# A fused attention and maxout FFN kernel: first loads through hardware queues with casts on chip, another pace for the FFN units, other PSUM banks

## The chip, the cores and the metric

The program runs on one core of one Trainium2 chip. The metric is the device time of one execution in microseconds (us), as a median of several runs. The "span" of a profiled run goes from its first to its last instruction; it is 1.7 us shorter than the time in the two profiled runs compared first, and 1.7 to 2.0 in the others.

Names: PE is the matrix engine (TensorE), DVE the vector engine, ACT the scalar engine (ScalarE), POOL is GpSimd, SP the sync engine. PE writes its sums into PSUM; the kernel's three PSUM pools below hold eight banks (3 + 2 + 3).

## The reference

```python
# q, k, v: 8 batches x 8 heads x 576 tokens x 64; beacon_k, beacon_v: 16 more keys per head
k_all = concat([beacon_k, k]); v_all = concat([beacon_v, v])        # 592 keys
scores = q @ k_all.T / 8, causal over the last 576 keys
a = exp(scores - max); a /= a.sum() + 1e-9
x = (a @ v_all), heads side by side                                  # 4608 tokens x 512
h = maximum(maximum(x @ w1, x @ w2), x @ w3)                         # 4608 x 768
out = h @ w_out                                                      # 4608 x 512, FP32
```

Inputs and output are FP32; the kernel computes in BF16 with FP32 sums.

## The kernel before

The program is a fixed order of instructions for each engine, written by one Python function. It works in these units:

- A *pair* is two heads of one batch: four pairs to a batch, 32 in all. Its scores are made in six *chunks* of key rows. In each chunk PE makes one score tile for each of the two heads, ACT takes the exponential, and DVE or POOL masks the diagonal.
- Before its first chunk, a pair's queries and keys are turned on PE (28 small transposes) and copied from PSUM by DVE into `qz` and `kT`.
- A *quad* is two pairs. Its *value passes* (six, in three steps) come in chunks 2 to 4 of the next quad's first pair.
- The FFN works on blocks of 512 tokens. A block has 22 *units*: 18 of the first layer (4 matmuls each) and 4 of the second (6 each). Units are laid between the chunks, so that PE has work while ACT makes exponentials. A block is ready only when the batch that it ends in has had its value passes.

The parts that matter here, with cuts marked:

```python
sc_psum  = ...tile_pool(name="sc_psum",  bufs=3, space=PSUM)   # scores and transposes
pv_psum  = ...tile_pool(name="pv_psum",  bufs=2, space=PSUM)
ffn_psum = ...tile_pool(name="ffn_psum", bufs=3, space=PSUM)
...
def load_qk(b, hs):                     # cast FP32 -> BF16 by the transfer, issued from GpSimd
    nc.gpsimd.dma_start(out=q_sb[:, hs, :], in_=q[b, hs]...)
    nc.gpsimd.dma_start(out=k_sb[BP:KP, hs, :], in_=k[b, hs]...)
    nc.gpsimd.dma_start(out=k_sb[0:BP, hs, :], in_=beacon_k[b, hs]...)
...
def emit_all():
    for pi in range(2): load_qk(0, ...pair pi...)
    for t in range(n_kt): load_v(0, t); build_mask(t)
    for pi in range(2, PPB): load_qk(0, ...)
    load_weights()                      # then batch 1: load_qk(1, all heads), load_v(1, t)
    ...
    emit_transposes(0)
    for p in range(NPAIR):
        b, pi = divmod(p, PPB)
        for c in range(6):
            emit_scores(p, c)
            if p >= 2 and p % 2 == 0 and 1 <= c <= 3:
                emit_pv(p // 2 - 1, c - 1)
            if c == 4 and pi == 0:
                ready = b - 1           # batch b - 1 is complete: its block may start
            if c == 4 and p + 1 < NPAIR:
                emit_transposes(p + 1)
            if b > 0:
                allowed += 0.95         # FFN units allowed so far
                while done[0] + 1 <= allowed and ... units[done[0]][0] <= ready:
                    emit_ffn(ready, allowed)
    # after the last pair: its quad's value passes, then all the units that are left
```

The softmax here doesn't subtract the row's maximum and nothing guards it: scores larger than these inputs give would overflow.

## Time and profile before

Time: 372.36 us (371.84 to 372.39), span 371.0 us. I cut the span at the first exponential of each batch, read in ACT's timeline:

| stretch | before, us |
|---|---|
| start to batch 0's first exponential | 8.8 |
| batch 0 | 36.0 |
| batch 1 | 37.6 |
| batches 2 to 7, mean of one | 39.7 |
| after the last exponential (44 units, last value passes, output) | 50.6 |

The page's second part of the kernel before has one digit for each fortieth of the span (9.3 us): the busy share of the engine in tenths (9 is 90% or more); for PEclk the clock that was granted to PE, in tenths of full speed; for DMA the mean share of the 16 transfer engines.

```profile
PE   2895499999999998989997999799998999899994
ACT  1754156645664666464746375555646365521110
PEclk9996599999999999989998999989998999999998
DMA  7999907761876168610953078703952001300404
```

PE is nearly always busy after 50 us, and the start is loaded with transfers. But a busy PE need not be a useful one. The chain of waits of the kernel before, in order of time (start, us, what), cut to where batches begin:

```profile
28.39 14.20 DMA k_sb<-in_beacon_k_dram
51.00 3.56 PE fps L300 x16
88.04 4.42 PE fps L300 x20
125.92 5.29 PE fps L300 x24
166.34 6.15 PE fps L300 x28
207.13 6.15 PE fps L300 x28
247.48 7.01 PE fps L300 x32
288.52 7.88 PE fps L300 x36
```

These are first-layer matmuls in one uninterrupted run: 4, 5, 6, 7, 7, 8 and 9 units. Each batch frees one block of 22 units, the pace is 24 chunks of 0.95, so 22.8. The units run out before a batch ends, 0.8 earlier each time, nothing is ready until the fifth chunk of the next batch, and then the allowance is caught up in one burst.

What PE does when units have run out is in the windows of the kernel before (stretch, its length, then busy time and number of instructions of PE, of PE's weight loads, of DVE, ACT and POOL, then the granted clock, where 1.00 is full, DMA share, GB/s). The first line is a stretch with units, for comparison:

```profile
188.00:190.00 2.00, 2.00 (x36) 1.24 (x35) 1.52 (x4) 0.58 (x2) 0.61 (x2) 1.00 0.00 0
198.00:200.00 2.00, 0.80 (x22) 0.46 (x15) 1.69 (x3) 0.50 (x3) 1.07 (x4) 1.00 0.71 227
200.00:202.00 2.00, 1.69 (x32) 1.06 (x34) 0.00 (x0) 1.38 (x5) 1.03 (x4) 0.74 0.00 0
202.00:204.00 2.00, 2.00 (x40) 0.97 (x36) 0.46 (x1) 1.72 (x4) 0.30 (x1) 0.50 0.00 0
```

PE idles 1.2 of 2 us, then its clock is halved, and in the last line it is "fully busy" at half the clock. The Trainium skill warns of this: "Perfetto Trace Analysis", in the note at its head, calls matmul busy time a bad metric for how close a kernel is to its limit.

Last, what PE waited for, from the waits of the kernel before (us in total, times, longest):

```profile
PE sc L176 <- DMA q_sb<-in_q_dram: 9.5, 2, 4.8
PE sc L215 <- DVE kT L193: 7.1, 9, 1.1
PE sc L215 <- ACT at_sb L223: 6.4, 20, 0.6
PE sc L184 <- DMA k_sb<-in_beacon_k_dram: 4.7, 2, 3.3
```

The first and last lines are the loads of batches 0 and 1. The third is a wait for a score bank that an exponential has still to empty.

### The profile page before, as it was taken

To read this page: it belongs to the slowest core of one execution; us is meant where nothing else is said; L and a number is where in the kernel's file an instruction comes from. 1 tells how busy PE (TensorE), PEld (TensorE's weight loads), DVE (VectorE), ACT (ScalarE), POOL (GpSimd) and SP (SyncE) were. 2 spreads that over 40 slices of the span, in tenths; PEclk is the share of its full clock that TensorE was granted. 3 is DMA by queue.
4 is the path that set the end of the run, shared out by engine and by line. 5 is a ranking of instruction groups with operands and counts; after the bars stand their busy time and mean duration, and the time that the engine had idled before them with its cause. 6 is when DMAs were issued, how large, how long until landed. Compare 5 with 4: busy or idle time off the path is not lost.

```text
span 371.0 us, 9819 instructions
## 1 busy us (share of the span) xinstructions
PE 333.5 (90%) x4064; PEld 178.9 (48%) x4064; DVE 185.9 (50%) x334; ACT 186.2 (50%) x503; POOL 163.9 (44%) x441
## 2 busy tenths in 40 slices
PE   2895499999999998989997999799998999899994
PEld 1452255545555555554554555354554555444441
DVE  3444156555646554545553656444563646245452
ACT  1754156645664666464746375555646365521110
POOL 8965127552765356533844165534654143300000
PEclk9996599999999999989998999989998999999998
DMA  7999907761876168610953078703952001300404
GB/s 78 128 186 204 137 4 116 59 104 35 122 52 110 30 98 79 96 44 7 155 48 104 2 110 67 137 2 43 133 81 59 0 2 31 87 2 0 113 2 113
DMA packets 60812, 27.64 MB, mean 75 GB/s; under 512 B 42976, under 2 KB 56160, under 8 KB 60768
## 3 DMA queue, kind: packets, MB, share of 16 engines
q0 software_dynamic: 55008, 17.58, 43.9%
q1 hardware_dynamic: 5760, 9.44, 9.1%
q8 instruction: 32, 0.52, 0.6%
q14 instruction: 12, 0.10, 0.1%
HBM read 35.13 MB, written 9.44 MB: 120 GB/s over the span
## 4 chain that ended last, share of the span: by engine, by line
PE 75%; ACT 7%; DMA 7%; POOL 6%; DVE 2%; issue 1%; POOLq 0%; ACTq 0%
PE fps L300 35%; PE fps L317 11%; PE sc L215 10%; PE pv L261 10%; PE sc L300 4%; ACT at_sb L223 4%; DMA k_sb<-in_beacon_k_dram 4%; PE sc L184 3%; PE sc L176 2%; DMA w_sb<-in_moe_w_dram 2%; PE sc L317 1%; POOL v_sb L137 1%; DVE kT L193 1%; ACT lnd L271 1%; DMA v_sb<-in_v_dram 1%
## 5 line engine op out<-in xcount | busy, mean ns | idle before, releaser
L223 ACT ACTIVATE at_sb<-sc 128x288 bf16<-128x288 f32 (+4 forms) x384 | 130.3, 404 | 91.4 <-PE sc L215 90.5
L239 POOL TENSOR_SCALAR_AFFINE_SELECT at_sb<-at_sb 128x57 bf16<-128x57 bf16 (+1 forms) x336 | 94.3, 300 | 145.2 <-ACT at_sb L223 139.7
L300 PE MATMUL fps<-xT,w_sb 128*128 128x512 bf16 x576 | 140.4, 380 | 0.0
L310 DVE TENSOR_TENSOR hT<-hT,fps 128x512 bf16<-128x512 bf16 x96 | 65.9, 686 | 56.9 <-PE fps L300 42.8
L300 PEld LDWEIGHTS <-w_sb 128*128 128x128 bf16 x648 | 59.5, 98 | 61.3 <-issue 0.8
L215 PEld LDWEIGHTS <-kT 128*128 128x128 bf16 (+1 forms) x384 | 36.6, 105 | 52.1 <-DVE kT L193 11.9
L308 ACT CAST hT<-fps 128x512 bf16<-128x512 f32 x48 | 28.1, 585 | 59.5 <-PE fps L300 49.5
L278 DVE TENSOR_TENSOR xT<-pv,recip 128x288 bf16<-128x288 f32 x64 | 27.5, 454 | 53.1 <-ACT recip L273 41.5
L317 PE MATMUL fps<-w_out_sb,hT 128*128 128x512 bf16 x192 | 46.5, 380 | 0.0
L137 POOL DMA_DIRECT2D v_sb<-in_v_dram x40 | 33.9, 851 | 6.0 <-DMA w_out_sb<-in_moe_w_out_dram 2.6
L261 PE MATMUL pv<-at_sb,v_sb 128*32 128x288 bf16 (+4 forms) x1280 | 36.0, 254 | 0.3 <-ACT lnd L271 0.2
L215 PE MATMUL sc<-qz_104,kT 128*128 128x288 bf16 (+2 forms) x96 | 30.2, 317 | 5.4 <-DVE kT L193 5.4
L261 PEld LDWEIGHTS <-v_sb 128*32 128x32 bf16 (+1 forms) x1280 | 27.5, 103 | 15.3 <-issue 13.0
L325 DVE COPY y<-fps 128x512 f32<-128x512 f32 x32 | 22.1, 691 | 24.3 <-PE fps L317 21.8
L215 PE MATMUL sc<-qz_106,kT 128*128 128x288 bf16 (+2 forms) x96 | 30.0, 313 | 3.1 <-ACT at_sb L223 2.8
L215 PE MATMUL sc<-qz_110,kT 128*128 128x288 bf16 (+2 forms) x96 | 28.6, 298 | 4.0 <-ACT at_sb L223 3.5
L215 PE MATMUL sc<-qz_108,kT 128*128 128x288 bf16 (+2 forms) x96 | 28.8, 301 | 2.3 <-DVE kT L193 1.7
L317 PEld LDWEIGHTS <-hT 128*128 128x128 bf16 x216 | 20.2, 98 | 21.5 <-DVE hT L310 0.9
L193 DVE COPY kT<-sc 128x592 bf16<-128x592 bf16 x32 | 24.8, 775 | 5.1 <-PE sc L184 4.2
L176 PE MATMUL sc<-ident,q_sb 96*64 96x96 bf16 x384 | 15.3, 218 | 10.3 <-DMA q_sb<-in_q_dram 9.5
L184 PE MATMUL sc<-ident,k_sb 74*64 74x74 bf16 x512 | 15.8, 205 | 6.1 <-DMA k_sb<-in_beacon_k_dram 4.7
L261 PE MATMUL pv<-at_sb,ones 128*32 128x288 bf16 (+4 forms) x640 | 20.4, 260 | 1.0 <-DVE xT L278 0.8
(35 smaller groups left out, 183.9 us busy)
## 6 DMA issues: line engine op xcount, KB each, us to landing
out_dram<-y SPq DMA_DIRECT2D x24, 192.0 KB, 2.5
q_sb<-in_q_dram POOLq DMA_DIRECT2D x7, 576.0 KB, 6.2
k_sb<-in_k_dram POOLq DMA_DIRECT2D x7, 576.0 KB, 9.1
v_sb<-in_v_dram POOLq DMA_DIRECT2D x24, 128.0 KB, 4.1
out_dram<-y SPq DMA_DIRECT2D x24, 128.0 KB, 2.4
w_sb<-in_moe_w_dram POOLq DMA_DIRECT2D x12, 192.0 KB, 7.8
out_dram<-y SPq DMA_DIRECT2D x24, 64.0 KB, 2.2
v_sb<-in_v_dram POOLq DMA_DIRECT2D x8, 112.0 KB, 3.8
```

What stands on the lines that cost most here:

```text
L137: nc.gpsimd.dma_start(out=v_sb[lo : lo + n, t], in_=v[b, :, t0 : t0 + n, :].rearrange("h p d -> p h d"),)
L184: nc.tensor.transpose(kT_ps[64 * e : 64 * e + 64, r, :], k_sb[:, head(g, j0 + e), r * D : (r + 1) * D], ident[0:KP, 0:KP],)
L193: nc.vector.tensor_copy(kT, kT_ps.rearrange("d r p -> d p r"))
L215: nc.tensor.matmul(ps[0:n, 0 : nr * w].rearrange("k (r p) -> k r p", p=w), kT[:, 128 * t : 128 * t + n], qz[p % NQZ][e][:, r0:r1, p0:QP], ...
L223: nc.scalar.activation(out=at_sb[0:n, t, j0 + e, r0:r1, p0:QP], in_=sc[e][0:n, 0 : nr * w].rearrange("k (r p) -> k r p", p=w), func=AF.Exp ...
L239: nc.gpsimd.affine_select(out=view, in_=view, compare_op=ALU.is_ge, fill=0.0, base=QR * p0 + r0 - k_tok[t], pattern=[[1, nr], [QR, p1 - p0 ...
L261: nc.tensor.matmul(ps[32 * j : 32 * j + 32, :, p0:QP], lhsT, at_sb[0:n, t, j, rs, p0:QP], start=(t == 0), stop=(t == n_kt - 1), tile_posit ...
L278: nc.vector.tensor_mul(xs.rearrange("c (r p) -> c r p", p=QP), ps, state["recip", hf])
L300: nc.tensor.matmul(ps, w_in[i][:, ct, 128 * ft : 128 * (ft + 1)], xT[:, ct, t0 : t0 + TOKB], start=(ct == 0), stop=(ct == n_ct - 1),)
L308: nc.scalar.copy(hT[:, ft, :], ps)
L310: nc.vector.tensor_max(hT[:, ft, :], hT[:, ft, :], ps)
L317: nc.tensor.matmul(ps, hT[:, ft, 128 * tt : 128 * (tt + 1)], w_out_sb[:, ft, :], start=(ft == 0), stop=(ft == n_ft - 1),)
```

## The change

Its intent: start sooner, use the time in which batch 1 is loaded, and feed PE more evenly. In parts:

1. Batch 0's queries and keys come as FP32 through the hardware queues (issued from SP and ACT) and are cast on DVE and ACT.
2. First-layer weights are loaded in two column halves.
3. After batch 0 come its second quad's value passes and ten FFN units, before batch 1 begins.
4. The pace is 22 units a batch; batch 1 gets 7, so that 5 are always left over for the first chunks of the next batch.
5. Score banks 4 instead of 3, FFN banks 2 instead of 3; the next pair's transposes come after the fourth chunk instead of the fifth (batch 0's use FFN banks).

```diff
-    sc_psum = ...(name="sc_psum", bufs=3)      +    ... bufs=4
-    ffn_psum = ...(name="ffn_psum", bufs=3)    +    ... bufs=2
+    def load_qk_first(pi):
+        q32 = stage_pool.tile([QP, 2, QR * D], FP32); k32 = stage_pool.tile([KP, 2, KR * D], FP32)
+        other = nc.scalar if pi < 2 else nc.sync
+        nc.sync.dma_start(out=q32, ...); other.dma_start(out=k32[BP:KP], ...)
+        nc.sync.dma_start(out=k32[0:BP], ...)
     def emit_transposes(p):
+        if b == 0:
+            nc.vector.tensor_copy(q_sb[:, pair_heads(pi), :], q32)
+            nc.scalar.copy(k_sb[:, pair_heads(pi), :], k32)
     def emit_all():
-        load_weights()
+        load_w_in(0, d_ff // 2); load_w_in(d_ff // 2, d_ff); load_w_out()
...
-                if c == 4 and p + 1 < NPAIR:
+                if c == 3 and p + 1 < NPAIR and p + 1 != PPB:
                     emit_transposes(p + 1)
                 if b > 0:
-                    allowed += 0.95
+                    per_batch = len(units) // n_tokb - (allowed0 + 5 if b == 1 else 0)   # 22; 7 for b == 1
+                    allowed += per_batch / (PPB * len(chunks))
...
+            if p == PPB - 1:                       # after batch 0
+                for step in range(3): emit_pv(p // 2, step)
+                ready = 0; allowed = allowed0      # 10
+                while done[0] < allowed: emit_ffn(ready, allowed)
+                emit_transposes(p + 1)
```

More of the change, by code (lines that the diff above doesn't have):

```diff
@@ L65, in head, with pair_heads @@
         return n_quad * j + g
+    def pair_heads(pi):
+        g, j0 = pi // 2, 2 * (pi % 2)
+        return slice(head(g, j0), head(g, j0 + 1) + 1, n_quad)
     const = ctx.enter_context(tc.tile_pool(name="const", bufs=1))
@@ L72 @@
     xT = xt_pool.tile([128, n_ct, n_tokens], BF16)
+    stage_pool = ctx.enter_context(tc.tile_pool(name="stage", bufs=2))
     load_pool = ctx.enter_context(tc.tile_pool(name="load", bufs=3))
@@ L79 @@
     ffn_y = ctx.enter_context(tc.tile_pool(name="ffn_y", bufs=3))
-    sc_psum = ctx.enter_context(tc.tile_pool(name="sc_psum", bufs=3, space=PSUM))
+    sc_psum = ctx.enter_context(tc.tile_pool(name="sc_psum", bufs=4, space=PSUM))
     pv_psum = ctx.enter_context(tc.tile_pool(name="pv_psum", bufs=2, space=PSUM))
-    ffn_psum = ctx.enter_context(tc.tile_pool(name="ffn_psum", bufs=3, space=PSUM))
+    ffn_psum = ctx.enter_context(tc.tile_pool(name="ffn_psum", bufs=2, space=PSUM))
     ident = const.tile([128, 128], BF16)
@@ L125, in load_qk @@
         )
+    stage = {}
+    def load_qk_first(pi):
+        hs = pair_heads(pi)
+        q32 = stage_pool.tile([QP, 2, QR * D], FP32, name="q32")
+        k32 = stage_pool.tile([KP, 2, KR * D], FP32, name="k32")
+        stage[pi] = q32, k32
+        other = nc.scalar if pi < 2 else nc.sync
+        nc.sync.dma_start(
+            out=q32, in_=q[0, hs].rearrange("h (p r) d -> p h (r d)", r=QR)
+        )
+        other.dma_start(
+            out=k32[BP:KP], in_=k[0, hs].rearrange("h (p r) d -> p h (r d)", r=KR)
+        )
+        nc.sync.dma_start(
+            out=k32[0:BP], in_=beacon_k[0, hs].rearrange("h (p r) d -> p h (r d)", r=KR)
+        )
     def load_v(b, t):
@@ L140, in load_v, with load_w_in @@
         )
-    def load_weights():
+    def load_w_in(f0, f1):
         for i, w_ap in enumerate((moe_w1, moe_w2, moe_w3)):
@@ L146, in load_weights, with load_w_out @@
             for j in range(4):
-                nc.gpsimd.dma_start(out=w_in[i][32 * j : 32 * j + 32], in_=wv[j])
+                nc.gpsimd.dma_start(
+                    out=w_in[i][32 * j : 32 * j + 32, :, f0:f1], in_=wv[j, :, :, f0:f1]
+                )
+    def load_w_out():
         nc.gpsimd.dma_start(
@@ L171, in emit_transposes, with turn @@
         g, j0 = pi // 2, 2 * (pi % 2)
-        q_sb, k_sb, _ = load_tiles(b)
-        qT_ps = sc_psum.tile([128, QR, QP], BF16, name="sc")
-        for r in range(QR):
-            for e in range(2):
-                nc.tensor.transpose(
-                    qT_ps[64 * e : 64 * e + 64, r, :],
-                    q_sb[:, head(g, j0 + e), r * D : (r + 1) * D],
-                    ident[0:QP, 0:QP],
-                )
-        kT_ps = sc_psum.tile([128, KR, KP], BF16, name="sc")
-        for r in range(KR):
-            for e in range(2):
-                nc.tensor.transpose(
-                    kT_ps[64 * e : 64 * e + 64, r, :],
-                    k_sb[:, head(g, j0 + e), r * D : (r + 1) * D],
-                    ident[0:KP, 0:KP],
-                )
+        kT = kt_pool.tile([128, KP, KR], BF16, name="kT")
+        state[p] = kT.rearrange("d p r -> d (p r)")
+        def turn(src, n, n_r):
+            pool, name = (ffn_psum, "fps") if b == 0 else (sc_psum, "sc")
+            ps = pool.tile([128, n_r, n], BF16, name=name)
+            for r in range(n_r):
+                for e in range(2):
+                    nc.tensor.transpose(
+                        ps[64 * e : 64 * e + 64, r, :],
+                        src[e][:, r * D : (r + 1) * D],
+                        ident[0:n, 0:n],
+                    )
+            return ps
+        q_sb, k_sb, _ = load_tiles(b)
+        qs, ks = ([t[:, head(g, j0 + e), :] for e in range(2)] for t in (q_sb, k_sb))
+        if b == 0:
+            q32, k32 = stage.pop(pi)
+            nc.vector.tensor_copy(q_sb[:, pair_heads(pi), :], q32)
+            nc.scalar.copy(k_sb[:, pair_heads(pi), :], k32)
+        q_ps = turn(qs, QP, QR)
+        k_ps = turn(ks, KP, KR)
         for e in range(2):
             hs = slice(64 * e, 64 * e + 64)
-            nc.vector.tensor_copy(qz[p % NQZ][e][hs], qT_ps[hs])
-        kT = kt_pool.tile([128, KP, KR], BF16, name="kT")
-        nc.vector.tensor_copy(kT, kT_ps.rearrange("d r p -> d p r"))
-        state[p] = kT.rearrange("d p r -> d (p r)")
+            nc.vector.tensor_copy(qz[p % NQZ][e][hs], q_ps[hs])
+        nc.vector.tensor_copy(kT, k_ps.rearrange("d r p -> d p r"))
     chunks = [(0, 0, RH), (0, RH, QR)] + [(t, 0, QR) for t in range(1, n_kt)]
@@ L356, in emit_all @@
         PPB = H // 2
-        for pi in range(2):
-            g, j0 = pi // 2, 2 * (pi % 2)
-            load_qk(0, slice(head(g, j0), head(g, j0 + 1) + 1, n_quad))
+        load_qk_first(0)
+        load_qk_first(1)
+        for t in range(n_kt):
+            build_mask(t)
         for t in range(n_kt):
             load_v(0, t)
-            build_mask(t)
-        for pi in range(2, PPB):
-            g, j0 = pi // 2, 2 * (pi % 2)
-            load_qk(0, slice(head(g, j0), head(g, j0 + 1) + 1, n_quad))
-        load_weights()
+        load_w_in(0, d_ff // 2)
+        load_w_in(d_ff // 2, d_ff)
+        load_w_out()
         load_qk(1, slice(0, H))
@@ L372, in emit_all @@
         allowed = 0.0
+        allowed0 = 10
         emit_transposes(0)
@@ L377, in emit_all @@
                 emit_scores(p, c)
-                if p >= 2 and p % 2 == 0 and 1 <= c <= 3:
+                if p != PPB and p >= 2 and p % 2 == 0 and 1 <= c <= 3:
                     emit_pv(p // 2 - 1, c - 1)
+                if c == 3 and p + 1 < NPAIR and p + 1 != PPB:
+                    if b == 0 and pi < 2:
+                        load_qk_first(pi + 2)
+                    emit_transposes(p + 1)
                 if c == 4 and pi == 0:
                     ready = b - 1
-                if c == 4 and p + 1 < NPAIR:
-                    emit_transposes(p + 1)
                 if b > 0:
-                    allowed += 0.95
-                    while done[0] + 1 <= allowed and done[0] < len(units) and units[done[0]][0] <= ready:
+                    per_batch = len(units) // n_tokb - (allowed0 + 5 if b == 1 else 0)
+                    allowed += per_batch / (PPB * len(chunks))
+                    while done[0] + 1 <= allowed and units[done[0]][0] <= ready:
                         emit_ffn(ready, allowed)
@@ L395, in emit_all @@
                 tiles.pop(b - 1)
+            if p == PPB - 1:
+                for step in range(3):
+                    emit_pv(p // 2, step)
+                ready = 0
+                allowed = allowed0
+                while done[0] < allowed:
+                    emit_ffn(ready, allowed)
+                emit_transposes(p + 1)
         for step in range(3):
@@ L399, in emit_all @@
         i = 0
-        tail = [(ffn_psum, "fps"), (sc_psum, "sc"), (pv_psum, "pv")]
+        tail = [(ffn_psum, "fps"), (sc_psum, "sc")]
         while done[0] < len(units):
-            pool, name = tail[i % 3]
             emit_ffn(B - 1, len(units), *tail[i % 2])
```

## The prediction

> **What bounds the kernel now.** The chain of waits gives PE 75% of the span. From the timeline: a first-layer FFN unit (4 matmuls) 0.863 us, a second-layer unit 1.295, a value pass 0.425, a pair's transposes about 0.75, its scores about 1.4. One batch with 22 FFN units is then about 33 us of warm PE work (estimate, my sum); the chain shows batches repeating every 40 to 41 us. The missing 7 us: each batch offers exactly 22 units, the old pace is 0.95 x 24 = 22.8 per batch, and no unit of the next block is ready until the fifth chunk. So units run out before the batch ends, and are caught up in bursts (16, 20, 24 ... 36 matmuls in the chain). Between 196.7 and 207.1 us there is attention alone: about 6 us of warm work in 10.4 us, and the granted clock in the windows falls to 0.50 at 202 to 204 us (0.50 and 0.65 at 160 to 164). The Trainium skill, "TensorE: Matmul & The Clock Gate", section "What's actually happening", says that an idle window halves the PE clock and busy time restores it; the trace agrees. About 4.5 us lost per batch.
>
> The start is the second loss: PE waits 4.8 us for batch 1's queries, 3.3 for its keys (waits by engine); batch 1 begins at 44.3 us, FFN at 51.
>
> **What the change does.**
> 1. The pace: 22 per batch with 5 units carried over, so units never run out. This is the main gain. I expect batches 2 to 7 at 35 to 36 us each instead of 40: about -28 us, of which about 10 return in the tail, which gets 11 more units.
> 2. Batch 1 keeps 7 units and half its value passes. It is bound by ScalarE and latency: about 26 us instead of 38; mostly displaced work.
> 3. Ten units (9 to 10 us) and the second quad's value passes (5 us) run between batches 0 and 1 and cover the waits for batch 1's loads. But batch 0 gets slower: the key cast on ScalarE (about 1.05 us, estimated from the 512-element cast at 585 ns) and the query cast on VectorE sit after the exponentials of the fourth chunk, and the last two chunks queue behind the transposes. I expect pairs 0 and 1 to take about 7 us instead of 6.1.
> 4. First scores: about 8 us, as before (8.35): the loads start sooner but add a cast, and the key issue follows ScalarE's table load (until 2.1 us).
> 5. Batch 1's first scores at about 53 us instead of 44, with 11 us more work done: a gain near 2 us.
> 6. Score banks 4: slightly fewer waits; FFN banks 2: small stalls behind the 1.7 us of query and key copies. About zero net. Weight halves: off the path.
>
> Sum: 53 + 26 + 6 x 35.3 + 55 = 346 us.
>
> **Prediction: 346 us, 80% range 338 to 356.** Faster by over 2%: 0.94; within 2%: 0.05; slower: 0.01.
>
> **Right if:** batch period near 35 us, no bursts of over 8 first-layer matmuls after the start, clock near 1.00 from batch 2 on; tail about 10 us longer; first scores near 8 us; batch 0 not faster. **Wrong if:** two FFN banks stall PE each chunk (period over 37 us); batch 1, thinly filled, runs at half clock (over 30 us); batch 1's keys land after 52 us.

## The result, and the profile after

Time: 345.58 us (345.07 to 345.70, four runs) against 372.36. The ratio is 0.9281, 95% interval 0.9265 to 0.9297. Here and below, a ratio is the mean time of one kernel's runs over that of the kernel before's runs of the same rounds, so it is not quite the ratio of the medians that are quoted. Runs which may be on different chips are compared by these ratios.

| stretch | before | after | difference |
|---|---|---|---|
| start to batch 0's first exponential | 8.8 | 9.8 | +0.9 |
| batch 0 (after: with 10 units and a quad's value passes more) | 36.0 | 43.5 | +7.6 |
| batch 1 (after: 7 units instead of 22, one quad's passes less) | 37.6 | 22.8 | -14.8 |
| batches 2 to 7, mean of one | 39.7 | 35.4 | 6 x -4.3 |
| after the last exponential (49 units instead of 44) | 50.6 | 55.6 | +5.0 |
| span | 371.0 | 343.9 | -27.1 |

Batches 2 to 7 make about 26 of the 27.1 us; the other rows together give little over 1 us.

The same rows of the page for the changed kernel (each slice now 8.6 us):

```profile
PE   1676897989999999999999999999999999999993
ACT  2675626875666557665757475647573765120210
PEclk9998799999999999999999999999999999999999
DMA  8999950991993189306940694059713100402204
```

The dents of PE and of its clock are gone from 50 us on. The windows of the changed kernel over three batches:

```profile
123.00:158.00 35.00, 34.07 (x489) 19.74 (x495) 20.56 (x36) 22.39 (x62) 19.76 (x58) 1.00 0.63 84
158.00:194.00 36.00, 35.02 (x494) 20.27 (x500) 20.59 (x37) 22.45 (x62) 20.59 (x58) 1.00 0.62 81
194.00:229.00 35.00, 34.02 (x488) 19.69 (x494) 20.36 (x36) 22.39 (x62) 19.68 (x58) 1.00 0.62 83
```

Every 35 to 36 us hold about 490 matmul records (this trace lacks some, see below), as 40 us held about 495 before, at the full clock. In the chain of waits of the changed kernel one burst is left, that of the ten units, and there is no other at a batch's start:

```profile
28.48 13.03 DMA k_sb<-in_k_dram
41.54 9.21 PE fps L332 x39
```

The first of these lines is not a wait for batch 1's keys: by the trace's landings they are there at 43.4 to 43.6 us, after the units have begun. The ten units have 40 matmuls, and the record of the first is missing; the profile puts the hole of 0.16 us down to this transfer. This profile has 4011 matmul records, every other profile of this document 4064.

What PE waits for now:

```profile
PE fps L208 <- DVE q_sb L219: 11.9, 4, 6.6
PE sc L247 <- DVE kT L226: 5.6, 7, 1.6
PE sc L247 <- ACT at_sb L255: 0.9, 3, 0.4
PE fps L332 <- DMA k_sb<-in_k_dram: 0.2, 1, 0.2
```

The waits for batch 1's loads are gone (the last line is the hole just named), and waits for score banks fell from 6.4 to 0.9 us. But there is a new one, the largest: 11.9 us for the cast of the queries, all in batch 0; 6.6 of it is the start, where the load itself is waited for. This is how that looks in the timeline of the changed kernel (start, length, engine, line, what, in brackets the idle time before and what ended it), for the first pair and for the hand-over from pair 0 to pair 1:

```profile
0.82 0.37 SPq L141 DMA_DIRECT2D q_119<-in_q_dram  x1
0.84 0.61 ACTq L144 DMA_DIRECT2D k_120<-in_k_dram  x1
5.86 0.72 DVE L219 CAST q_sb<-q_119 96x768 bf16<-96x768 f32 x1 [2.60 <-DMA q_119<-in_q_dram]
6.61 1.04 ACT L220 CAST k_sb<-k_120 74x1024 bf16<-74x1024 f32 x1 [4.52 <-DMA k_120<-in_beacon_k_dram]
7.71 0.71 PE L208 MATMUL fps<-ident,k_sb 74*64 74x74 bf16 x16 [0.38 <-ACT k_sb L220]
9.29 0.42 PE L247 MATMUL sc<-qz_107,kT 128*128 128x288 bf16 x1 [0.87 <-DVE kT L226]
...
12.47 1.08 ACT L220 CAST k_sb<-k_125 74x1024 bf16<-74x1024 f32 x1
12.98 0.55 DVE L219 CAST q_sb<-q_124 96x768 bf16<-96x768 f32 x1
13.58 0.69 PE L208 MATMUL fps<-ident,q_sb 96*64 96x96 bf16 x12 [1.81 <-DVE q_sb L219]
15.09 0.83 ACT L255 ACTIVATE at_sb<-sc 128x210 bf16<-128x210 f32 x4 [1.54 <-PE sc L247]
```

And the same first pair in the kernel before, where the transfer casts:

```profile
1.42 0.76 POOL L115 DMA_DIRECT2D q_sb<-in_q_dram  x1 [0.40 <-issue]
4.74 0.69 PE L176 MATMUL sc<-ident,q_sb 96*64 96x96 bf16 x12 [4.74 <-DMA q_sb<-in_q_dram]
6.78 0.70 PE L184 MATMUL sc<-ident,k_sb 74*64 74x74 bf16 x16 [1.35 <-DMA k_sb<-in_beacon_k_dram]
8.35 0.42 PE L215 MATMUL sc<-qz_104,kT 128*128 128x288 bf16 x1 [0.87 <-DVE kT L193]
```

The hardware transfer of the queries is issued 0.6 us sooner and its data is there 1.1 us later (5.86 against 4.74). But the first scores wait for the keys, and these are there at 6.6 to 6.8 us in both kernels: it is their cast, 1.04 us, that puts PE's key transposes at 7.71 instead of 6.78 us and the first scores at 9.29 instead of 8.35. One profile of each is not the whole range: in the ten profiled runs of this document that load batch 0 this way, the first scores start at 8.4 to 9.3 us, in the four that load it as before at 8.3 to 8.4. In batch 0 then, ACT, which makes the exponentials, also casts keys for 1.08 us a pair, and stands idle for 1.54 us because the fifth chunk's scores wait on PE behind the transposes.

### The profile page after: what moved, and what is told of

It is laid out like the page before. It is cut to its first block, busy times and chain, and to the rows that moved or that the text cites. A ratio compares the mean times of both kernels' runs of the same rounds, so it can differ in the third digit from the quotient of the medians.

```text
span 343.9 us, 9797 instructions
## 1 busy us (share of the span) xinstructions
PE 311.6 (91%) x4011; PEld 174.4 (51%) x4064; DVE 185.8 (54%) x338; ACT 187.0 (54%) x507; POOL 162.0 (47%) x441
## 4 chain that ended last, share of the span: by engine, by line
PE 73%; DVE 9%; DMA 8%; POOL 5%; issue 3%; ACT 1%; DVEq 0%
PE fps L332 32%; PE fps L349 12%; PE sc L247 10%; PE pv L293 10%; PE sc L332 5%; DMA k_sb<-in_k_dram 4%; PE sc L208 3%; DVE kT L226 2%; DVE hT L342 2%; DMA v_sb<-in_v_dram 2%; DMA w_sb<-in_moe_w_dram 2%; PE sc L349 2%; POOL w_sb L171 2%; DVE xT L310 1%; POOL at_sb L271 1%
## 5 line engine op out<-in xcount | busy, mean ns | idle before, releaser
L255 ACT ACTIVATE at_sb<-sc 128x288 bf16<-128x288 f32 (+4 forms) x384 | 129.0, 406 | 77.4 <-PE sc L247 74.7
L247 PEld LDWEIGHTS <-kT 128*128 128x128 bf16 (+1 forms) x384 | 38.6, 106 | 46.7 <-DVE kT L226 6.5
L349 PE MATMUL fps<-w_out_sb,hT 128*128 128x512 bf16 x171 | 42.7, 380 | 1.6 <-issue 1.3
L310 DVE TENSOR_TENSOR xT<-pv,recip 128x288 bf16<-128x288 f32 x64 | 27.7, 454 | 29.6 <-ACT recip L305 22.4
L293 PE MATMUL pv<-at_sb,v_sb 128*32 128x288 bf16 (+4 forms) x1280 | 33.1, 242 | 0.2 <-ACT lnd L303 0.2
L247 PE MATMUL sc<-qz_107,kT 128*128 128x288 bf16 (+2 forms) x96 | 28.4, 300 | 4.5 <-DVE kT L226 3.6
L293 PEld LDWEIGHTS <-v_sb 128*32 128x32 bf16 (+1 forms) x1280 | 25.8, 98 | 12.6 <-issue 11.3
L247 PE MATMUL sc<-qz_111,kT 128*128 128x288 bf16 (+2 forms) x96 | 28.8, 301 | 2.2 <-DVE kT L226 1.8
L247 PE MATMUL sc<-qz_113,kT 128*128 128x288 bf16 (+2 forms) x96 | 28.7, 301 | 0.3
L247 PE MATMUL sc<-qz_109,kT 128*128 128x288 bf16 (+2 forms) x96 | 28.4, 302 | 0.2 <-DVE kT L226 0.2
L226 DVE COPY kT<-sc 128x592 bf16<-128x592 bf16 x28 | 21.7, 775 | 0.9
L208 PEld LDWEIGHTS <-q_sb 96*64 96x64 bf16 x384 | 10.7, 114 | 18.9 <-DVE q_sb L219 13.2
L293 PE MATMUL pv<-at_sb,ones 128*32 128x288 bf16 (+4 forms) x640 | 18.7, 246 | 0.6 <-DVE xT L310 0.6
L332 PE MATMUL sc<-xT,w_sb 128*128 128x512 bf16 x71 | 18.4, 379 | 0.1
```

The source lines that it names most:

```text
L226: nc.vector.tensor_copy(kT, k_ps.rearrange("d r p -> d p r"))
L247: nc.tensor.matmul(ps[0:n, 0 : nr * w].rearrange("k (r p) -> k r p", p=w), kT[:, 128 * t : 128 * t + n], qz[p % NQZ][e][:, r0:r1, p0:QP], ...
L255: nc.scalar.activation(out=at_sb[0:n, t, j0 + e, r0:r1, p0:QP], in_=sc[e][0:n, 0 : nr * w].rearrange("k (r p) -> k r p", p=w), func=AF.Exp ...
L293: nc.tensor.matmul(ps[32 * j : 32 * j + 32, :, p0:QP], lhsT, at_sb[0:n, t, j, rs, p0:QP], start=(t == 0), stop=(t == n_kt - 1), tile_posit ...
L310: nc.vector.tensor_mul(xs.rearrange("c (r p) -> c r p", p=QP), ps, state["recip", hf])
L332: nc.tensor.matmul(ps, w_in[i][:, ct, 128 * ft : 128 * (ft + 1)], xT[:, ct, t0 : t0 + TOKB], start=(ct == 0), stop=(ct == n_ct - 1),)
```

## The experiments

Twelve kernels ran; all gave correct results, and each was timed in three rounds beside the kernel before. The total came out as predicted, so the question was whether its parts did. The prediction put nearly the whole gain on the pace (theory A). Rival B puts it on the loads, the units during the loads and the banks.

### 1. The pace alone, on the kernel before

```diff
-                    allowed += 0.95
+                    per_batch = len(units) // n_tokb - (5 if b == 1 else 0)
+                    allowed += per_batch / (PPB * len(chunks))
```

> The kernel before with the pace alone: 22 units a batch, 17 in batch 1, so that 5 are always left. Theory A (the feeding of PE is the main gain): batches 2 to 7 fall from 39.7 to 35.5-36.5 us each, batch 1 from 37.7 to about 33, the tail grows by about 4 us; time about 348 us (345 to 351). Rival B (the loads, the units during the loads and the banks carry the gain): at least 362 us, batches still over 38 us.

Measured: 358.52 us against 373.19, ratio 0.9602 (0.9576 to 0.9628). Batches 2 to 7 took 36.9 us each (before 39.7), batch 1 35.1, the tail (all after the last exponential) 55.5. The clock record has no cold stretch (one at half clock) between 49.8 us and the end of the span, as its page shows:

```profile
PEclk9998579999999999999999999999999999999999
```

So the pace alone is worth 4.0% of the 7.2%: more than half, as A has it, but it stops 1.6 us a batch short of the changed kernel. Neither theory was right by itself.

### 2. The changed kernel without the carry

```diff
-  (allowed0 + 5 if b == 1 else 0)
+  (allowed0 if b == 1 else 0)
```

> The changed kernel with the 5 carried units spent in batch 1 (12 there instead of 7), pace 22 unchanged. Theory A: each batch now begins with five chunks of attention alone and a catch-up of 4 to 5 units; batches 2 to 7 grow from 35.6 to 38-39 us, with granted clock under 1.00 there; batch 1 about 3 us longer, tail about 4 shorter; time 358 to 366 us. Rival A2 (it is the rate 22 instead of 22.8, not the carry): within 3 us of 345.6. Rival B: within 3 us of 345.6.

Measured: 347.70 us, ratio 0.9318 (0.9292 to 0.9343). Batches 2 to 7 took 35.9 us against 35.4. A miss for theory A, while A2 and B, which said within 3 us of 345.6, held: the five chunks without units and the burst of four units at each batch's fifth chunk cost 0.5 us a batch, not 3, and the clock stayed at full speed. The carry is worth about 0.4% of the time.

### 3. The changed kernel with the old pace

```diff
-  per_batch = len(units) // n_tokb - (allowed0 + 5 if b == 1 else 0)
+  per_batch = 22.8 - (allowed0 if b == 1 else 0)
```

> The changed kernel with the old rate, 22.8 units a batch and nothing carried (batch 1: 12.8), so that units run out before every batch's end, earlier each time, as in the kernel before. Theory A as predicted (running out costs about 4.5 us a batch): 360 us or more. Theory C2 (with four score banks the attention that is left alone runs near PE's rate, so running out costs little; the run without the carry lost only 2 us): batches at 36 to 36.6 us, time 347 to 351 us.

Measured: 357.02 us, ratio 0.9585 (0.9564 to 0.9607). Batches 2 to 7 took 37.5 us each: 36.5 in batch 2, 38.4 at most, in batch 4, and 37.4 in batch 7. Batches 2 to 7 do 132 units in all of these kernels, so nothing is displaced among them. The bursts of the kernel before are back; the first and the last in this run's chain of waits:

```profile
84.41 4.46 PE fps L332 x20
271.78 8.06 PE fps L332 x36
```

Both expectations missed: taking the pace away costs 3.0% (0.9585 less 0.9281), and most of that is not the missing carry (0.4%) but the rate of 22.8, with which units end earlier in each batch. Why that costs so much more than the missing carry (2.1 against 0.5 us a batch) these runs don't show. Half clock is not the reason here: the clock record of this run has no cold stretch between 39 and 305 us.

### 4. Old banks

```diff
-  sc_psum bufs=4, ffn_psum bufs=2
+  sc_psum bufs=3, ffn_psum bufs=3
```

> The changed kernel with three score banks and three FFN banks, as before. New theory C (the fourth score bank is worth 1.6 us a batch, which the run with the pace alone lacks: its batches take 37.15 us against 35.57): batches 2 to 7 at 37 us or more, PE waits for exponentials (ScalarE) back at some 5 us in total instead of 1.2; time 354 to 358 us. My prediction on record (banks about zero net): 344 to 347 us.

Measured: 354.09 us, ratio 0.9506 (0.9475 to 0.9538). The waits of this run:

```profile
PE fps L208 <- DVE q_sb L219: 10.9, 4, 5.9
PE sc L247 <- ACT at_sb L255: 7.0, 22, 0.6
```

The waits for exponentials are back at 7.0 us (0.9 with four banks), as theory C expected. Batches 2 to 7 take 36.2 us, 0.9 more than with four score banks and less than C's 37; batch 1 takes 3.1 us more. The time is at the lower edge of C's range. The swap of one bank from FFN to scores is worth 2.2% of the time (0.9506 less 0.9281). "About zero net" in the prediction was wrong.

### 5. Transposes after the fifth chunk

```diff
-  if c == 3 and p + 1 < NPAIR and p + 1 != PPB:
+  if c == 4 and p + 1 < NPAIR and p + 1 != PPB:
```

> The changed kernel with the next pair's transposes after the fifth chunk, as before, instead of after the fourth; four score banks kept. If the earlier transposes are what saves 1.6 us a batch: batches at 37 us, time 354 to 358 us. Theory C (the bank does it): batches at 35.6 to 36.2 us, time 345 to 349 us; batch 0 may gain about 1 us a pair, as the casts no longer hold up the fifth chunk's scores.

Measured: 351.24 us (349.25 to 352.53), ratio 0.9440 (0.9406 to 0.9474); the profiled run was the fastest of the four, at 349.25. In it batches 2 to 7 take 35.6 us (0.3 more), batch 1 1.6 more, and batch 0's pairs 7.3 instead of 6.8. PE's waits for `kT` rise from 5.6 to 11.3 us:

```profile
PE sc L247 <- DVE kT L226: 11.3, 13, 1.6
```

So the earlier transposes are worth 1.0 (that fastest run) to 1.6% (the mean of the four); in the profiled run over half of it lies outside the steady batches, where the slower three lost time is not known; theory C's range for the batches held, its range for the time and my hope for batch 0 missed.

### 6. The old loads in the changed kernel

```diff
-        load_qk_first(0); load_qk_first(1); masks; load_v(0, t)
+        load_qk(0, pair 0), load_qk(0, pair 1); load_v(0, t) and masks; load_qk(0, pairs 2 and 3)
-            nc.vector.tensor_copy(q_sb[...], q32); nc.scalar.copy(k_sb[...], k32)
```

> The changed kernel with batch 0's queries and keys loaded as before (cast by the transfer, issued from GpSimd, no casts on chip). My theory: the casts cost more than they save: first scores at 8.3-8.5 us instead of 9.3, pairs 0 and 1 about 5.8-6.1 us instead of 6.8; batch 1's first scores at 49 to 51 us instead of 53; time 342 to 344 us. Rival B (the hardware loads help): batch 0 or the loads of batch 1 later than in the changed kernel, time 347 us or more.

Measured: 340.42 us, ratio 0.9127 (0.9085 to 0.9168). The first exponential comes at 8.8 us instead of 9.8 (8.9 to 9.8 in the ten profiled runs with the hardware loads), pairs 0 and 1 take 5.5 us instead of 6.8, and batch 1's first exponential comes at 48.2 us instead of 53.3. Batches 2 to 7 take 35.36 us in both. The first-named part of the change costs 1.5% of the time.

### 7. Casts earlier

```diff
+                if b == 0 and c == 1 and pi + 1 < PPB:
+                    cast_first(pi + 1)          # instead of just before the transposes
```

> The changed kernel, hardware loads kept, but the casts of a pair are put after the second chunk of the pair before, not after its fourth. If the place of the casts (between the exponentials and the transposes) is what makes batch 0 slower than with the old loads: pairs 0 and 1 at 5.5-6.0 us instead of 6.8, batch 1's first exponentials at 50-51 us instead of 53.3, time 342 to 343.5 us. If the loads themselves are at fault (they land later): pairs stay near 6.8 us and the time at 345 to 346.

Measured: 343.90 us, ratio 0.9224 (0.9198 to 0.9251). Pairs 0 and 1 take 6.4 us: the place of the casts explains 0.4 of the 1.4 us a pair that separates the changed kernel from the old loads. The first exponential stays late, at 9.65 us. What remains is close to the cast that ACT still makes in every pair (1.08 us); the cast itself on ACT was not moved to another engine, so that last step is argued, not shown.

### 8. No units between batches 0 and 1

```diff
-        allowed0 = 10
+        allowed0 = 0                    # batch 1 gets 17 instead of 7
```

> The changed kernel with no unit between batches 0 and 1; batch 1 gets 17 instead of 7. The trace of the changed kernel shows batch 1's keys landed by 41.5 us, just when the units began, so my theory: there is no wait left to cover, batch 1's first scores at about 44 us, batch 1 about 28 us instead of 22.8 (PE has slack in it); time 341 to 343 us. Rival (the units cover the loads): PE waits over 3 us for batch 1's keys and the time is 346 us or more.

Measured: 343.38 us, ratio 0.9206 (0.9164 to 0.9248). The waits of this run show what the ten units had to cover:

```profile
PE sc L247 <- DVE kT L226: 4.8, 6, 1.2
PE sc L208 <- DMA k_sb<-in_beacon_k_dram: 1.3, 1, 1.3
```

PE waits 1.3 us for batch 1's keys (they land at 42.4 us, not by 41.5 as I had written). Batch 1's first exponential comes at 44.3 us, and batch 1 with 17 units takes 29.0 us. The sum of the two is 2.8 us less than with ten units up front. Units laid in one block feed PE alone (9.2 us for the ten); in batch 1 they fill gaps that are there anyway (6.2 us more for ten more units). The second quad's value passes stayed between the batches in this run, and were not taken away alone in any. But with them and without units batch 1's first exponential comes no later than in the kernel before (44.3 against 44.8 us), so they fill time in which PE waited before.

### 9. Weights in whole rows

```diff
-        load_w_in(0, d_ff // 2); load_w_in(d_ff // 2, d_ff)
+        load_w_in(0, d_ff)
```

> The changed kernel with the first-layer weights loaded in whole rows, 12 transfers instead of 24. My prediction (off the path): the same within 1 us, 344.5 to 346.5. Rival (the halves let the ten units start earlier): the first FFN unit waits for weights and starts over 1 us later than 41.5 us; 347 us or more.

Measured: 345.73 us, ratio 0.9284 (0.9245 to 0.9323): the same, as predicted. But the landings in the trace show that the halves are not free: with whole rows batch 1's keys land at 39.1 us, with halves at 43.6. The difference arises at the issue: the trace has batch 1's queries issued by POOL at 23.2 us with whole rows, at 27.7 with halves. A weight transfer occupies POOL for about 0.55 us in either form, so 24 of them take 13.3 us and 12 take 6.7. The ten units and the value passes hide that difference.

### 10 and 11. The same 22 units in 19 chunks, none at the start, or none at the end

```diff
-                    allowed += per_batch / (PPB * len(chunks))
+                    elif ci >= 5:                 # none at the start; the twin has ci < 19
+                        allowed += per_batch / 19
```

> The changed kernel with the 22 units of each of batches 2 to 7 all in its last 19 chunks; the first five chunks (which hold three value steps) get none. Theory C3 (chunks without units are cheap where value passes stand in for them): batches at 35.8 to 36.3 us, time 347 to 351 us. Rival (any five chunks without units cost the same): the same time as its twin within 1 us.

> The twin: 22 units in the first 19 chunks, none in the last five (which hold no value passes). Theory C3: scores and exponentials alone go at ScalarE's pace, batches at 36.7 to 37.5 us, time 352 to 358 us, at least 4 us over the other twin. Rival: the same as the other twin within 1 us.

Measured: 367.34 us with none at the start (363.59 to 368.24, ratio 0.9836, 0.9778 to 0.9893, verdict unclear at 2%), 356.50 with none at the end (ratio 0.9573, 0.9540 to 0.9607). The order is the opposite of what theory C3 said, but the first twin was spoilt by something that I had not thought of. Its waits of DVE:

```profile
DVE y L357 <- DMA out_dram<-y: 11.3, 5, 3.1
```

In that order the four second-layer units of a block follow each other within 7 us (123.2 to 130.1 us in one batch), and their results find no free output buffer: DVE waits 11.3 us in total for output transfers (in the changed kernel no such wait is among DVE's longest), and PE waits 9.9 us for DVE. That covers part of the 17 us that its batches 2 to 7 lose against the changed kernel. The pair of runs doesn't decide C3. The twin with none at the end, which has no such wait, lost 1.8 us a batch, while five chunks without units at the start in experiment 2 lost 0.5. That fits C3 (chunks with value passes need units less than chunks of scores alone), but the two runs differ in more than the place, so it stays open.

### 12. What the runs point to, together

```diff
   the changed kernel's pace, banks and place of the transposes, with
+  batch 0 loaded as in experiment 6, weights in whole rows,
+  batch 1's queries, keys and values before the second layer's weights, allowed0 = 3
```

> What the runs point to: pace, banks and transposes of the changed kernel; batch 0's queries and keys loaded as before, without casts; weights in whole rows, batch 1's queries, keys and values loaded before the second layer's weights; three units up front instead of ten, 14 in batch 1. Expected: batch 1's keys land by 39 us, its first exponentials at 41 to 42 us, batch 1 about 27 us, time 336 to 339 us, against 340.4 with the old loads alone. Wrong if batch 1's keys still come at 42 us or later: then 340 or more.

Measured: 336.34 us (335.88 to 336.94), ratio 0.9024 (0.8998 to 0.9050). Batch 1's first exponential comes at 41.1 us, batch 1 takes 26.0 us. This beats both kernels.

## Why the prediction was right or wrong

The time was right (346 predicted, 345.58 measured), and so was the mechanism that the prediction named first. Its sum, in the trace's time, point by point:

| term | predicted, us | measured, us |
|---|---|---|
| batch 1's first scores | 53 | 52.95 |
| batch 1 | 26 | 22.8 |
| batches 2 to 7, each | 35.3 | 35.4 |
| rest | 55 | 55.6 after the last exponential |
| sum | 346 | 343.9 span, 345.6 time |

The one term of the sum that was mis-sized is batch 1, 3.2 us too long. I had feared a half clock there; the trace shows the clock at 1.00. Part of that error is hidden because I set a span against a time, which is 1.7 us longer here.

1. *The pace is the main gain*: right. Alone it gives 4.0% of 7.2%, and taking it away from the changed kernel costs 3.0%. But the prediction credited it with the whole 4.4 us a batch; alone it gives 2.7 us (39.7 to 36.9). Of the other 1.6 us, taking the bank back costs 0.9 and the late transposes 0.3, parts that I had written off or not priced; 0.4 is not assigned by any run. The step that failed inside it is "with 5 units carried over, so units never run out": without the carry units do run out in every batch, and it costs 0.5 us a batch, not 4.4. The rate matters more than the carry (old rate: 2.1 us a batch).
2. *About 10 us return in the tail, which gets 11 more units*: wrong. The tail has 5 more units and is 5.0 us longer. I had counted units by the allowance (159 by the end of batch 7); the old kernel could only do what was ready (154).
3. *Half clock*: present as described, but not the main part. In batches 2 to 7 of the kernel before the clock record has four cold stretches of 3.4 us, which cost at most half of that each (an estimate: 7 us in all, of the 26 us that these batches gained). The Trainium skill, "TensorE: Matmul & The Clock Gate", section "What's actually happening", gives a window of about 3.4 us; the record's cold stretches here are 3.4, 6.8 and 17.1 us, so it agrees.
4. *Batch 0 not faster, pairs at 7 us instead of 6.1*: right, 6.8. Experiment 6 shows that the loads with casts cost 1.5% of the time.
5. *First scores at about 8 us*: wrong in this run, 9.3; 8.4 to 9.3 over the ten profiled runs with these loads. The step was that "the loads start sooner", which they do, and that this pays for the cast. In this run the keys were there no sooner than before (6.6 us; 5.7 to 6.7 over the ten runs), and their cast of 1.04 us came on top. My reason for a late key transfer was wrong too: its issue, at 0.84 us, did not wait for ACT's table load.
6. *Ten units and value passes cover the waits for batch 1's loads, a gain near 2 us*: the size of the start's gain came out (all rows of the table but batches 2 to 7 give about 1.3 us, the bank's 3.1 us in batch 1 among them), but the ten units are not what earns it; their sign is wrong. Without them the waits are 1.3 us and the kernel is about 0.8% faster.
7. *Score banks about zero net*: wrong. Together with the FFN bank given up for it, the fourth score bank is worth 2.2%. I had costed it by PE's waits in the profile (6.4 us for exponentials), and not asked what an evenly paced batch would wait for. The feared stalls with two FFN banks do not show as waits for a bank: before FFN matmuls the profile has only 25 holes of 0.16 us, 4.0 us in total, and they are missing records and not waits: the unit after each has 3 records instead of 4, or 5 instead of 6, and no other profile with two FFN banks has such a hole.
8. *Weight halves off the path*: right.

So the total was right partly because errors cancelled: the pace was over-credited, the bank and the place of the transposes under-credited, and the start was worse than said. That the sum fell within half a us of the measured time is luck.

## What to carry to other kernels

Count filler work by what is ready, not by what the pace allows, and set the pace to the supply: 0.8 units a batch too many cost 3 to 4% here. A filler placed where the main work already leaves gaps is worth more than the same filler in a block that hides one wait. Price a faster load by when its data can be used, cast included, and not by when it is issued.

## What the Trainium skill lacked or had wrong

- "DMA: Bandwidth & Descriptors", section "Issuing engine by pattern", says that the sync and scalar paths are generally faster than GpSimd's. The first queries, 288 KB of FP32 through SP, could be used 5.0 us after the issue (4.4 to 5.2 over ten profiled runs); the same data cast by the transfer and issued from GpSimd, 3.3 us. The section "Issuing engines are not separate DMA queues" of the same page fits better: other queues save issue time only. It was 0.37 against 0.76 us of issuing here. Other transfers were under way beside it in both cases, issued closer together in the one (all of the first two pairs by 2.3 us) than in the other (by 5.7 us), so the path itself was not measured alone.
- No page read gives the time for which a transfer occupies GpSimd when it is issued there. Here a weight transfer took about 0.55 us, whether of 96 or of 192 KB, so that 24 instead of 12 of them brought the next loads 4.5 us later (queries issued at 27.7 against 23.2 us, keys landed at 43.6 against 39.1).
- "TensorE: Matmul & The Clock Gate" says under its trace caveats that clock events can't be fully trusted. One more case: the windows give a clock of 1.00 for the first 30 us of both kernels, while matmuls of 288 columns start 0.23 us apart there (at 9.51 and 9.74 us in the changed kernel) and 0.12 to 0.13 us apart later (53.08 and 53.20 us). The record seems to begin with its first event, at 26.9 us in the kernel before and 28.5 us in the changed kernel; earlier figures of the clock are no evidence.
